# Two tiles for the first K^T V, one undivided last copy, and a different chunk order in one product

## Chip, cores, metric

One core of one Trainium2 chip. The metric is the device time of one execution in microseconds (us). The kernel before took 285.2 us (median of 3 runs, 285.11 to 285.89). Matrix products are in bf16, inputs and outputs in fp32. Medians below are of all runs listed; ratios are the mean time of one kernel's fast runs over the mean of the other's fast runs of the same rounds, so not quite the ratio of the medians that are quoted.

## The reference

Linear attention without softmax, a norm per head, then a two-layer product with ELU between:

```python
kv  = np.einsum('bhsd,bhse->bhde', k, v)          # q, k, v: 8 x 8 x 576 x 64
out = np.einsum('bhsd,bhde->bhse', q, kv)
rms = np.sqrt(np.mean(out * out, axis=-1, keepdims=True) + 1e-06)
x   = (out / rms * g_norm)  # -> transposed to 4608 x 512
h   = x @ w_in                                     # 512 x 2048
g   = np.where(h > 0, h, np.exp(np.minimum(h, 0)) - 1)
return g @ w_out                                   # 2048 x 512
```

## The kernel before

Tokens go in nine groups of 512 (NT = 9, groups 0 to 8). The four chunks of 128 rows that make up a group's x^T are called chunks 0 to 3; each holds two heads. A, V are ACT and DVE. PSUM is handed out by tags: "A" and "B" are one pair of banks each, "m" is a pool of two single banks, "x" another one of two. An allocation from a pool whose buffers are all taken waits for the last reader of the buffer it gets.

The start of batch 0 (cuts marked):

```python
    def chunk_kv(kv_ps, c):
        kv_mm(0, [kv_ps[:, s, :] for s in range(2)], c % 2, (c // 2,))

    def chunk_kv_out(kv_ps, c, eng):
        rows, cols = slice(c // 2 * 64, c // 2 * 64 + 64), slice(c % 2 * 64, c % 2 * 64 + 64)
        copy_on(eng, kv_sb[rows, 0, c % 2], kv_ps[rows, :, cols])
    # ...
    g_ps = pair("A", "g_ps")
    kv_ps = pair("B", "kv_ps")
    # ... first casts; transposed q in a tile of "m"
    mean = pair("A", "mean")[:, 0, :]
    chunk_kv(kv_ps, 0)
    chunk_kv_out(kv_ps, 0, V)
    chunk_kv(kv_ps, 2)
    chunk_kv_out(kv_ps, 2, V)
    chunk_y(0, single("x", "y_ps"))
    chunk_square(0)
    idle(1, mean)                      # filler matmul, keeps the tensor engine busy
    chunk_y(2, single("x", "y_ps"))
    chunk_square(2)
    idle(1, mean)
    mean_mm(sq0[0], mean)
    r = r_tile()
    inv_t(r[:, 0, :], mean)            # Ln, then Exp, on ACT
    ps = turned_q(0, 1, "m")
    q_t_out(0, 1, V, ps, slice(0, 8))
    mean = single("m", "mean")
    mean_mm(sq0[2], mean)
    nc.scalar.activation(r[:, 1, :], mean, AF.Ln, bias=eps_col)
    kv_ps = pair("B", "kv_ps")
    h_ps = [pair("A", "h_ps")]
    chunk_kv(kv_ps, 1)
    # ...
```

Group 1's first products, and the tail. `mm1` runs `mm1_part` over all four chunks for its two tiles, then the ELU; `last_columns` computes the last 128 rows of the output in two halves of 256 columns:

```python
    for i, tag in enumerate("mBAmBAm"):
        if i < 4:
            mm1(1, i, tag)()
    # ...
    def last_columns():
        for n in range(2):
            cols = slice(n * 256, n * 256 + 256)
            ps = single("m", "o_ps")[:, 0:256]
            # ... 16 matmuls into ps
            o = outp.tile([P, 2, DM], FP32, name="o_sb", tag="o")[:, 0, 0:256]
            if n == 0:
                nc.scalar.copy(o, ps)
            else:
                nc.scalar.copy(o[:, 0:128], ps[:, 0:128])
                nc.vector.tensor_copy(out=o[:, 128:256], in_=ps[:, 128:256])
            last_store(J - 1, o, cols)     # one store from ACT's queue, one from SyncE's
```

Of the kernel before, what the change touches and what calls it, by code (L numbers as in the profile page):

```python
# [16 lines left out]
def kernel(  # L17
# [13 lines left out]
    nc = tc.nc  # L31
# [11 lines left out]
    V, A, Q = nc.vector, nc.scalar, nc.gpsimd  # L43
# [64 lines left out]
    def copy_on(eng, out_, in_):  # L108
        if eng is nc.scalar:
            nc.scalar.copy(out_, in_)  # L110
        else:
            eng.tensor_copy(out=out_, in_=in_)  # L112
# [16 lines left out]
    def single(tag, name):  # L129
        pool = ps_x if tag == "x" else ps_m2  # L130
        return pool.tile([P, 512], FP32, name=name, tag=tag)

    def pair(tag, name):
        if tag in ("x", "m", "mx"):
            return [single(t, name) for t in (tag + tag)[:2]]
        return ps_m1.tile([P, 2, 512], FP32, name=name, tag=tag)
# [14 lines left out]
    def kv_mm(b, kv_ps, u, ls=range(2)):  # L151
        for j in range(RK):
            for s in range(2):
                rows = slice(s * 64, s * 64 + 64)
                for l in ls:
                    nc.tensor.matmul(  # L156
                        kv_ps[s][l * 64 : l * 64 + 64, u * 64 : u * 64 + 64],
                        lhsT=bf["k", b][rows, 2 * l + u, j, :],
                        rhs=bf["v", b][rows, 2 * l + u, j, :],
                        start=(j == 0),  # L160
                        stop=(j == RK - 1),
                    )
# [180 lines left out]
    def elu(T, i, ps, relu):  # L343

        parts = [(0, 2, ps)]
        if isinstance(ps, list):
            parts = [(a, a + 1, ps[a].unsqueeze(1)) for a in range(2)]
        e = mlpt.tile([P, 2, G], BF16, name="elu_e", tag="elu_e")
        for lo, hi, h in parts:
            nc.scalar.activation(e[:, lo:hi, :], h, AF.Exp)  # L350

        def freed():
            r = mlpt.tile([P, 2, G], BF16, name="elu_h", tag="elu_h", bufs=2)
            for lo, hi, h in parts:
                nc.scalar.activation(r[:, lo:hi, :], h, AF.Relu)  # L355
            parts[:] = [(0, 2, r)]

        if relu and relu != "later":
            freed()

        def rest():
            nc.vector.tensor_scalar(  # L362
                out=e, in0=e, scalar1=1.0, scalar2=1.0, op0=ALU.min, op1=ALU.subtract
            )
            for lo, hi, h in parts:
                nc.vector.tensor_tensor(  # L366
                    out=gT[T][:, 2 * i + lo : 2 * i + hi, :],
                    in0=e[:, lo:hi, :],
                    in1=h,
                    op=ALU.add if relu else ALU.max,  # L370
                )

        return (freed, rest) if relu == "later" else rest

    def g_tile(T):
        gT[T] = mlpg.tile([P, FC, G], BF16, name="gT", tag="gT")

    def mm1_part(T, i, ps, cs, cols=slice(0, 512), last=True):
        for a in range(2):
            f = 2 * i + a  # L380
            for n, c in enumerate(cs):
                nc.tensor.matmul(  # L382
                    (ps[a] if isinstance(ps, list) else ps[:, a, :])[:, cols],
                    lhsT=w_in_sb[:, c, f * P : f * P + P],
                    rhs=xT[T][:, c, cols],
                    start=(c == 0),
                    stop=(last and n == len(cs) - 1),
                )

    def mm1(T, i, tag, relu=False):  # L390
        if i == 0:
            g_tile(T)
        ps = pair(tag, "h_ps")
        mm1_part(T, i, ps, range(KC))
        return elu(T, i, ps, relu)
# [27 lines left out]
    def last_store(j, o, cols):  # L423
        rows = out_dram.rearrange("(b p j) f -> b p j f", b=B, j=RK)
        for h, eng in enumerate((nc.scalar, nc.sync)):
            b, jj = slot_of(NT - 1, 2 * j + h)
            eng.dma_start(out=rows[b][:, jj, cols], in_=o[h * 64 : h * 64 + 64])
# [5 lines left out]

    def last_columns():

        for n in range(2):
            cols = slice(n * 256, n * 256 + 256)
            ps = single("m", "o_ps")[:, 0:256]
            for f in range(FC):
                nc.tensor.matmul(  # L440
                    ps,
                    lhsT=gT[NT - 1][:, f, (J - 1) * P : J * P],
                    rhs=w_out_sb[:, f, cols],
                    start=(f == 0),
                    stop=(f == FC - 1),
                )
            o = outp.tile([P, 2, DM], FP32, name="o_sb", tag="o")[:, 0, 0:256]
            if n == 0:
                nc.scalar.copy(o, ps)
            else:  # L450
                nc.scalar.copy(o[:, 0:128], ps[:, 0:128])  # L451
                nc.vector.tensor_copy(out=o[:, 128:256], in_=ps[:, 128:256])  # L452
            last_store(J - 1, o, cols)

    def mm2_half(T, i):
# [2 lines left out]
    def store(T, half):  # L458
        rows = out_dram.rearrange("(b p j) f -> b p j f", b=B, j=RK)
        o = o_sb[T, half]  # L460
        for h in range(2):
            hs = slice(h * 64, h * 64 + 64)
            (b0, j0), (b1, j1) = (slot_of(T, 4 * half + 2 * t + h) for t in range(2))
            if b0 == b1:
                nc.sync.dma_start(out=rows[b0][:, j0 : j1 + 1 : 2, :], in_=o[hs])
            else:
                nc.sync.dma_start(out=rows[b0][:, j0, :], in_=o[hs, 0, :])
                nc.sync.dma_start(out=rows[b1][:, j1, :], in_=o[hs, 1, :])
# [62 lines left out]
    def turned_q(b, u, tag):  # L531

        ps = as_bf16(single(tag, "qt_ps"))
        q_t_mm(b, u, range(8), ps)
        return ps

    def first_cast(name, cs, eng, js):
        copy_on(eng, bf[name, 0][:, cs[0] : cs[-1] + 1 : 2, js, :], first[name][:, :, js, :])
# [7 lines that stand above are left out]
# [38 lines left out]
    kv_ps = pair("B", "kv_ps")  # L584
# [5 lines left out]
    ps = turned_q(0, 0, "m")  # L590
# [2 lines left out]
    q_t_out(0, 0, V, ps, slice(0, 8))  # L593
    first_cast("v", (0,), A, high)
    first_cast("v", (0,), V, low)
    mean = pair("A", "mean")[:, 0, :]
    chunk_kv(kv_ps, 0)
    chunk_kv_out(kv_ps, 0, V)
    chunk_kv(kv_ps, 2)
    chunk_kv_out(kv_ps, 2, V)  # L600
    chunk_y(0, single("x", "y_ps"))
# [8 lines left out]
# [7 lines that stand above are left out]
# [14 lines left out]
    mean = single("m", "mean")  # L631
# [34 lines left out]
    for tag, j0 in (("A", 0), ("B", 2)):  # L666
        ps = pair(tag, "o_ps")
# [4 lines left out]
    for u in range(2):  # L672
        n = Turned(1, u)
# [3 lines left out]
        kv_ps = [single("x", "kv_ps") for _ in range(2)]  # L677
# [32 lines left out]
    at = attention(2)  # L710
    freed, rest = {}, {}
    for i, tag in enumerate("mBAmBAm"):
        if i < 4:
            mm1(1, i, tag)()
        else:
            freed[i], rest[i] = mm1(1, i, tag, "later")
        if i == 3:
            at["kv"]()
        if i == 4:
            at["se0"]()  # L720
            freed[4]()
            at["sum0"]()
            at["inv0"]()
        if i == 5:
            at["mul0"]()
            store(0, 0)
            freed[5]()
        if i == 6:
            rest[4]()
            rest[5]()  # L730
    ps = pair("B", "h_ps")
# [13 lines left out]
    ps = pair("A", "o_ps")  # L745
# [61 lines left out]
    for i in (1, 3, 4, 5):  # L807
        mm2_half(NT - 1, i)
    last_columns()


# [28 lines left out]
```

## Time and profile before

| | before |
|---|---|
| time, median of 3 | 285.2 us |
| span of the profiled execution | 283.3 us, granted clock 1.0 |
| tensor engine busy | 97% of the span |
| share of the tensor engine in the chain that ended last | 96% |

The first rows of the profile's page give the busy time of each engine. The chain that ended last is followed back from the end; an engine that is nearly all of the chain can only be helped where it stands still. The lines for this are in the prediction below.

### The profile page before, as it was taken

The page shows a single profiled execution, that of the slowest core. Times are in us where ns is not written, and L with a number is a line of the kernel's source. Part 1 is how long each engine was busy: PE and PEld are TensorE (multiplying, and loading weights), DVE is VectorE, ACT ScalarE, POOL GpSimd, SP SyncE. Part 2 cuts the span into 40 slices and gives each one's busy share as a digit, 9 for nine tenths or more (in the row PEclk, how much of TensorE's full clock was granted, in tenths as well). Part 3 has the DMA queues.
Part 4 walks back from the last instruction along what each step waited for, and adds up shares of the span by engine and source line. Part 5 has one row for each costly group of instructions (what it writes and reads, how often), then busy time and mean ns, then how long its engine had stood idle before and what let it go on. Part 6 is the DMA issues. An engine that isn't in the chain of part 4 may idle for free.

```text
span 283.3 us, 5120 instructions
## 1 busy us (share of the span) xinstructions
PE 274.8 (97%) x2089; PEld 129.5 (46%) x2123; DVE 164.3 (58%) x222; ACT 141.4 (50%) x210; POOL 49.9 (18%) x89
## 2 busy tenths in 40 slices
PE   8899999999999999999999999999999999999994
PEld 3444444444544444444444444444444444444443
DVE  2459532867578647655775478537872787344600
ACT  3688359594667355425542555245533553333321
POOL 7743303332340033033003310000000000000000
PEclk9999999999999999999999999999999999999999
DMA  7999999999995979579627961602150235020222
GB/s 211 193 204 206 207 257 235 211 257 177 206 253 92 155 220 226 65 188 258 155 29 174 266 158 40 166 13 74 39 111 0 74 39 111 0 76 0 74 74 75
DMA packets 50571, 39.46 MB, mean 139 GB/s; under 512 B 30964, under 2 KB 44020, under 8 KB 50548
## 3 DMA queue, kind: packets, MB, share of 16 engines
q0 software_dynamic: 15008, 21.30, 37.4%
q1 hardware_dynamic: 35136, 17.31, 29.1%
q10 hardware_dynamic: 404, 0.53, 0.5%
q8 instruction: 16, 0.26, 0.4%
q14 instruction: 7, 0.06, 0.1%
HBM read 36.70 MB, written 9.44 MB: 163 GB/s over the span
## 4 chain that ended last, share of the span: by engine, by line
PE 96%; DVE 1%; issue 1%; ACT 1%
PE o_ps L403 43%; PE h_ps L382 42%; PE at L250 2%; PE kv_ps L529 2%; PE at L156 2%; PE o_ps L440 1%; PE h_ps L573 1%; PE qt_ps L174 1%; PE kv_ps L156 1%; PE mean L199 1%; PE y_ps L189 1%; DVE kv_sb L112 0%; DVE xT L212 0%; DVE qT L112 0%; ACT rT L634 0%
## 5 line engine op out<-in xcount | busy, mean ns | idle before, releaser
L403 PE MATMUL o_ps<-w_out_sb,gT 128*128 128x512 bf16 x548 | 128.8, 379 | 0.7 <-issue 0.2
L382 PE MATMUL h_ps<-xT,w_in_sb 128*128 128x512 bf16 (+1 forms) x540 | 126.6, 376 | 1.0
L350 ACT ACTIVATE elu_e<-h_ps 128x1024 bf16<-128x1024 f32 (+1 forms) x79 | 74.0, 952 | 89.4 <-PE h_ps L382 78.6
L403 PEld LDWEIGHTS <-gT 128*128 128x128 bf16 x560 | 54.4, 98 | 65.5 <-issue 0.4
L382 PEld LDWEIGHTS <-w_in_sb 128*128 128x128 bf16 x560 | 53.2, 98 | 61.3 <-issue 0.4
L366 DVE TENSOR_TENSOR gT<-elu_e,h_ps 128x1024 bf16<-128x1024 bf16 (+1 forms) x67 | 77.2, 1157 | 6.6
L362 DVE TENSOR_SCALAR elu_e<-elu_e 128x1024 bf16<-128x1024 bf16 x72 | 30.9, 430 | 65.0 <-ACT elu_e L350 64.8
L419 ACT COPY o_sb<-o_ps 128x512 f32<-128x512 f32 x32 | 18.3, 586 | 20.9 <-PE o_ps L403 20.2
L103 POOL CAST q_bf<-st_q 128x384 bf16<-128x384 f32 x36 | 18.5, 558 | 39.0 <-DMA st_q<-in_q_dram 33.6
L283 DVE TENSOR_REDUCE ss<-sq 128x16 f32<-128x1024 bf16 x14 | 17.1, 1219 | 6.8 <-ACT sq L277 6.8
L299 DVE TENSOR_TENSOR xs<-at,ss 128x1024 bf16<-128x1024 f32 x14 | 17.1, 1220 | 1.9 <-ACT ss L292 1.9
L277 ACT ACTIVATE sq<-at 128x1024 bf16<-128x1024 f32 x14 | 14.4, 1029 | 0.0
L212 DVE SCALAR_TENSOR_TENSOR xT<-y_ps,g_col,rT 128x512 bf16<-128x512 f32 (+1 forms) x10 | 6.2, 640 | 10.0 <-ACT rT L209 7.9
L339 POOL COPY gate<-qT 1x16 bf16<-1x16 bf16 x5 | 1.1, 218 | 57.7 <-DMA qT<-q_bf 57.7
L355 ACT ACTIVATE elu_h<-h_ps 128x1024 bf16<-128x1024 f32 (+1 forms) x12 | 9.3, 817 | 0.0
L90 POOL DMA_DIRECT2D v_bf<-in_v_dram x11 | 7.8, 713 | 4.2 <-DMA w_in_sb<-in_moe_w_in_dram 2.1
L156 PEld LDWEIGHTS <-k_bf 64*64 64x64 bf16 x576 | 6.4, 107 | 4.6 <-issue 4.1
L90 POOL DMA_DIRECT2D k_bf<-in_k_dram x11 | 7.7, 703 | 3.0 <-DMA w_in_sb<-in_moe_w_in_dram 2.3
L312 DVE TENSOR_SCALAR xT<-xT,g_col 128x1024 bf16<-128x1024 bf16 x14 | 6.7, 481 | 2.2 <-DMA xT<-xs 2.2
L250 PEld LDWEIGHTS <-qT 64*128 64x128 bf16 (+1 forms) x248 | 4.3, 97 | 6.1 <-issue 5.9
L366 DVE TENSOR_TENSOR gT<-elu_e,elu_h 128x1024 bf16<-128x1024 bf16 x9 | 6.6, 736 | 0.8
L452 DVE COPY o_sb<-o_ps 128x128 f32<-128x128 f32 x1 | 0.3, 292 | 11.3 <-ACT o_sb L451 11.3
(60 smaller groups left out, 102.4 us busy)
## 6 DMA issues: line engine op xcount, KB each, us to landing
st_q<-in_q_dram POOLq DMA_DIRECT2D x6, 1152.0 KB, 8.3
out_dram<-o_sb SPq DMA_DIRECT2D x24, 256.0 KB, 3.4
k_bf<-in_k_dram POOLq DMA_DIRECT2D x6, 576.0 KB, 10.3
v_bf<-in_v_dram POOLq DMA_DIRECT2D x6, 576.0 KB, 12.9
out_dram<-o_sb SPq DMA_DIRECT2D x19, 128.0 KB, 2.4
w_out_sb<-in_moe_w_out_dram POOLq DMA_DIRECT2D x4, 512.0 KB, 15.0
w_in_sb<-in_moe_w_in_dram POOLq DMA_DIRECT2D x2, 512.0 KB, 11.0
q_bf<-in_q_dram POOLq DMA_DIRECT2D x3, 288.0 KB, 13.4
```

Of the source, the lines that this page charges most:

```text
L90: eng.dma_start(out=dst.rearrange("p m j d -> p m (j d)"), in_=in_[:, ms, :])
L103: nc.gpsimd.tensor_copy(out=bf["q", b][:, u, js], in_=raw[b][:, u::2, js, :].rearrange("p l j d -> p j l d"),)
L156: nc.tensor.matmul(kv_ps[s][l * 64 : l * 64 + 64, u * 64 : u * 64 + 64], lhsT=bf["k", b][rows, 2 * l + u, j, :], rhs=bf["v", b][rows, 2 * ...
L277: nc.scalar.activation(sq, st["se", h], AF.Square)
L283: nc.vector.reduce_sum(out=ss, in_=st.pop(("sq", h)).rearrange("p l (m e) -> p (l m) e", e=D), axis=AX.X,)
L299: nc.vector.tensor_tensor(out=st["xs"][:, 2 * h : 2 * h + 2, :].rearrange("p i (l m e) -> p l i m e", l=2, e=D), in0=se_ps.rearrange("p l ...
L350: nc.scalar.activation(e[:, lo:hi, :], h, AF.Exp)
L362: nc.vector.tensor_scalar(out=e, in0=e, scalar1=1.0, scalar2=1.0, op0=ALU.min, op1=ALU.subtract)
L366: nc.vector.tensor_tensor(out=gT[T][:, 2 * i + lo : 2 * i + hi, :], in0=e[:, lo:hi, :], in1=h, op=ALU.add if relu else ALU.max,)
L382: nc.tensor.matmul((ps[a] if isinstance(ps, list) else ps[:, a, :])[:, cols], lhsT=w_in_sb[:, c, f * P : f * P + P], rhs=xT[T][:, c, cols] ...
L403: nc.tensor.matmul(o_ps[T, j], lhsT=gT[T][:, f, j * P : j * P + P], rhs=w_out_sb[:, f, :], start=(f == 0), stop=(f == FC - 1),)
L419: nc.scalar.copy(o_sb[T, half][:, j % 2, :], o_ps[T, j])
```

## The change

Its intent: (1) chunks 0 and 2 of K^T V get a tile each, so that chunk 2 need not wait for chunk 0's copy; the mean moves to pool "m" to make room. (2) Group 1's first product takes chunk 3, which is ready last, last for both of its tiles. (3) The last copy is one DVE copy of 256 columns, instead of 128 on ACT and 128 on DVE, which ran one after the other.

```diff
-        for n in range(2):
+        for n, eng in enumerate((A, V)):
 ...
-            if n == 0:
-                nc.scalar.copy(o, ps)
-            else:
-                nc.scalar.copy(o[:, 0:128], ps[:, 0:128])
-                nc.vector.tensor_copy(out=o[:, 128:256], in_=ps[:, 128:256])
+            copy_on(eng, o, ps)
 ...
-    mean = pair("A", "mean")[:, 0, :]
+    mean = single("m", "mean")
     chunk_kv(kv_ps, 0)
     chunk_kv_out(kv_ps, 0, V)
+    kv_ps = pair("A", "kv_ps")
     chunk_kv(kv_ps, 2)
 ...
-        if i < 4:
+        if i == 0:
+            g_tile(1)
+            ps = pair(tag, "h_ps")
+            mm1_part(1, 0, ps, (0, 2, 1), last=False)
+            mm1_part(1, 0, ps, (3,))
+            elu(1, 0, ps, False)()
+        elif i < 4:
             mm1(1, i, tag)()
```

## The prediction

> **What bounds the kernel now.** I read the page's busy shares first, then the chain that ended last, then that chain piece by piece in time at the three places the change touches: the start (7.8 to 20 us), the hand-over to group 1 (46 us) and the tail (after 279 us).
>
> ```profile
> PE 274.8 (97%) x2089; PEld 129.5 (46%) x2123; DVE 164.3 (58%) x222; ACT 141.4 (50%) x210; POOL 49.9 (18%) x89
> ...
> PE 96%; DVE 1%; issue 1%; ACT 1%
> ```
>
> The tensor engine is the chain for 96% of the span, at a granted clock of 9 tenths or more in every slice. No matmul of the real products is removed, and the instruction order on it is the same in both kernels apart from one block of eight matmuls. So only places where it stands still on the chain, and the tail after it, can give time. The chain by time names them; columns are start, duration and what:
>
> ```profile
> 7.85 0.48 PE kv_ps L156 x18
> 8.33 0.02 issue
> 8.36 0.29 DVE kv_sb L112
> 8.65 0.04 issue
> 8.69 0.38 PE kv_ps L156 x13
> ...
> 9.20 0.30 DVE kv_sb L112
> 9.51 0.10 issue
> 9.60 0.40 PE y_ps L189 x2
> 10.01 0.32 PE mean L529
> 10.33 0.21 PE mean L199
> 10.54 0.57 PE qt_ps L174 x16
> 11.11 0.32 PE mean L199
> 11.44 0.40 PE kv_ps L156 x18
> ...
> 46.49 0.65 PE h_ps L382 x3
> 47.14 0.01 issue
> 47.15 3.83 PE h_ps L382 x17
> ...
> 279.35 0.27 ACT o_sb L451
> 279.62 0.02 issue
> 279.64 0.29 DVE o_sb L452
> ```
>
> At 8.33 chunk 2's K^T V waits until chunk 0's result has been copied out of the same tile, 8.69 - 8.33 = 0.36 us. At 46.49, three matmuls of group 1's first product run and the fourth comes only at 47.15. The three start 216 ns apart (46.33, 46.54, 46.76 in the timeline), so the fourth was due at 46.98: 0.17 us lost to the last chunk of xT, whose scaling on DVE runs 46.34 + 0.75 = 47.09. After the last matmul, the two halves of the last copy run one after the other, not side by side: ACT 279.35 to 279.62, then DVE 279.64 to 279.94. The line of the DVE half says so:
>
> ```profile
> L452 DVE COPY o_sb<-o_ps 128x128 f32<-128x128 f32 x1 | 0.3, 292 | 11.3 <-ACT o_sb L451 11.3
> ```
>
> [...] between a full-array matmul at 11.04 and the 64x64 ones at 11.36 lie 0.32 us where 0.216 would do. This matters below. [...]
>
> **Part 1, different tiles at the start.** Removed: the wait of 0.36 us. Chunk 2's products can follow chunk 0's at about 8.16 (they issue 16 ns apart, the last of chunk 0 at 8.12) and end at 8.63 instead of 9.16; their inputs are there, as the queue's waits show the last of these two loads landed before 7.88. But not all of the 0.53 reaches the next steps:
> - y of chunk 0 now waits itself for the copy ending at 8.64, so starts at 8.69 instead of 8.88 and 8.97 for its two halves; it ends at 9.09 instead of 9.35, gain about 0.27. ACT's first square starts at 9.13 instead of 9.39.
> - The filler matmul behind it, and the change of tiling mode after that, hold y of chunk 2: start to start the old distances are 0.31 (8.97 to the filler's weights at 9.28) and about 0.32 (filler to 9.60), so y of chunk 2 comes at about 9.33 instead of 9.60, although its operand is ready at about 9.0.
> - The second filler and the first mean keep their distance: the mean at 9.90 instead of 10.165. Its Ln on ACT starts at 10.32 instead of 10.58 and ends, after 0.69, at 11.00 to 11.01 instead of 11.27.
>
> Now the new wait. The mean used to live in the pair A; A now holds chunk 2's product, so the mean takes a slot of the two-buffer pool "m". In order of allocation that pool gets: transposed q, mean 0, transposed q, mean of chunk 2. With two slots the fourth takes mean 0's slot and must wait until its Ln has read it. Released at about 11.00, plus about 0.04 to reach the tensor engine (the hop from DVE at 8.65 shows 0.04), it starts at 11.04. Before, the same matmul started at 11.04, in its place in the order. The transposes in front of it come 0.27 us early and then the tensor engine stands still for about that long. From there the next K^T V (11.36), its copy (11.88), y of chunk 1 (12.30) and the rest up to the first product at 19.86 are as before. So I put Part 1 at 0.00 us, with -0.05 to +0.12 as what the small hops leave open.
>
> **Part 2, the last chunk last.** Six matmuls without chunk 3, instead of three, run ahead: 46.33 + 6 x 0.216 = 47.63 is when the chunk is first needed, and it is ready at 47.14. The stall of 0.17 us goes. ACT's first exponential is at 48.11 before because ACT is copying o_ps until then (four copies from 46.21, 2.03 us); the first tile is done at about 47.63 + 0.38 = 48.01, so ACT loses nothing. The following products have slots free: pair B is copied out by 47.2 and A by 48.25, needed at about 48.06 and 49.8. From 47.15 on the chain is tensor-engine work with only 0.05 us pieces of issue, so the gain should reach the end: 0.17 us.
>
> **Part 3, the undivided copy.** Before: 279.35 to 279.94 = 0.59 us for two copies in series. After: one DVE copy of 128x256. [...] The hop from the tensor engine to DVE is 0.03 (8.33 to 8.36), the same as to ACT (279.32 to 279.35). Gain 0.59 - 0.425 = 0.16 us. The stores follow the copy in both kernels: issue at 279.97, landing and closing to 283.3, a fixed 3.3 us which shifts as a whole. The output slot's earlier stores had been waited for by 275.8, well ahead.
>
> **Sum.** 0.00 + 0.17 + 0.16 = 0.33 us off 285.2: 284.87, rounded to 284.9.
>
> **Rivals.** (a) The start pays in full: if mean 2 did not wait for the Ln, the 0.27 us that the mean gains would go through, or 0.36, the whole removed wait; then 284.5 to 284.6. For it: the wait is on the chain. Against: the slot order above, and Ln's own 0.69 us behind the first mean. (b) The start gets worse: the new wait releases later than I think, or the following K^T V waits twice, and mean 2 comes at 11.1 or 11.2: 285.0. For it: ACT's three instructions before that point follow each other almost without gaps. Against: y of chunk 0 is early by a wait that I read from the trace. (c) The gain at 47 us is given back: ACT's exponential of the first tile comes later, the m slots come free later, and a later product in m waits. Those two slots are read by DVE until 51.08, the next user comes at about 51.7, so 0.6 us is spare; if it still happened, 285.05. (d) DMA arrivals fix the start: chunk 3's v has landed by 12.55 at the latest and the first w_in pieces are used at about 13.9; they could swallow an earlier start but not cause a loss. It would make (a) smaller only.
>
> **Range and chances.** The three runs before spread from 285.11 to 285.89, more than the whole gain, so the median itself carries some 0.2 us. With the parts' spread (start -0.05 to +0.27, hand-over 0 to 0.2, tail 0.1 to 0.2) I take 284.5 to 285.3. Two per cent is 5.7 us; all the standing still at the three places adds up to 0.36 + 0.17 + 0.59 = 1.1 us, so neither a gain nor a loss of 2% is in reach: 0.01 and 0.01.
>
> **What would show it.** In the changed profile: chunk 2's K^T V at about 8.16 with no wait for DVE; y of chunk 0 at 8.69 and of chunk 2 at about 9.33; the second mean's matmul at about 11.04 with the tensor engine waiting for ACT's Ln in front of it, and the next K^T V at about 11.36 as before; eight matmuls 216 ns apart from about 46.33 with no wait for xT; one DVE copy of about 0.43 us at the end, and from its end to the span's end what it was before (283.3 - 279.94 = 3.36 us). I am wrong on Part 1 if the second mean starts before 10.95 or after 11.1, on Part 2 if the product after the block is not 0.17 earlier relative to its start, on Part 3 if the copy takes under 0.35 or over 0.5 us. A span of 282.95 or so (283.3 less 0.33) is the whole in one number.

The sum came to 0.00 + 0.17 + 0.16 = 0.33 us off 285.2, that is 284.9. Its 0.16 is 0.59 - 0.425, and 0.425 stands as the estimate, which no run had shown; the copy then took 425 ns in the changed kernel. The change of tiling mode stands with what the trace before shows: 0.32 us from the start of a 128x128 matmul to that of a 64x64 one (11.04 to 11.36), against 0.216 between the 128x128 ones at 46.33, 46.54 and 46.76.

## The result, and the profile after

The changed kernel took **285.42 us** (median of 6 runs, 284.91 to 286.71). In the same rounds the kernel before took 285.4 us (6 runs, 285.11 to 286.11). The ratio is 1.0004, 95% interval 0.9979 to 1.0028: the same. The predicted 284.9 us was missed, and the median lies outside the range of 284.5 to 285.3.

The profiled execution of the changed kernel happened to be its longest, 286.71 us with a span of 284.9, at a granted clock of 0.998; so the two profiles differ by 1.67 us while the medians do not. The first two lines of the page's parts on busy time and on the chain:

```profile
PE 276.2 (97%) x2123; PEld 128.9 (45%) x2123; DVE 164.9 (58%) x222; ACT 141.2 (50%) x209; POOL 49.2 (17%) x89
...
PE 88%; DMA 4%; ACT 3%; DVE 3%; issue 0%; SPq 0%; DVEq 0%
```

One ACT instruction is gone (210 to 209): the halved copy. The tensor engine's share of the chain fell from 96 to 88%; DMA, ACT and DVE took 10% between them. Following both traces side by side at the same instructions gives the account of the 1.67 us:

| place | after minus before |
|---|---|
| arrival of the first loads | +0.02 us |
| start, up to the first product (Part 1) | +0.01 |
| hand-over to group 1, 46 us (Part 2) | -0.17 |
| wait for x^T of group 2, 70 to 73 us | +1.57 |
| tail, from the last matmul to the end of the copy (Part 3) | +0.24 |

**Start.** The chain of the changed kernel from 7.8 us; columns are start, duration, what:

```profile
7.87 0.48 PE kv_ps L156 x24
8.35 0.02 issue
8.38 0.29 DVE kv_sb L112
8.67 0.04 issue
8.71 0.40 PE y_ps L189 x2
9.12 0.32 PE mean L525
...
10.35 0.70 ACT rT L208
11.04 0.04 issue
11.09 0.38 PE mean L199
11.46 0.40 PE kv_ps L156 x18
...
16.61 3.27 PE h_ps L569 x14
19.88 2.20 PE h_ps L382 x10
```

The wait between the two K^T V is gone, and y of chunk 0 starts at 8.71. But ahead of the second mean, at 11.09, the chain now goes through ACT's Ln, and from there everything is where it was.

**Hand-over.** The chain of the changed kernel at 46 us:

```profile
44.79 1.73 PE o_ps L403 x8
46.52 6.91 PE h_ps L382 x32
```

Where the chain before was broken after three matmuls, one piece of 32 follows.

**The wait at 70 us.** What the engines wait for between 60 and 74 us; columns are engine, written tile, line, releaser, then us in total, times, longest. Only the lines that concern xT are shown, first of the kernel before, then of the changed one:

```profile
DVE xT L312 <- DMA xT<-xs: 1.4, 1, 1.4
```

```profile
DVE xT L312 <- DMA xT<-xs: 3.1, 2, 1.8
PE h_ps L382 <- DVE xT L312: 1.2, 1, 1.2
PEld L382 <- DMA xT<-xs: 1.0, 1, 1.0
```

In the second, the transposed x of group 2 lands late, and the tensor engine waits for it, once through DVE and once directly. This is the largest difference of the two profiles, and no part of the change touches that place. Is it the change's doing?

**Tail.** The chain of the changed kernel at its end:

```profile
277.24 1.76 PE o_ps L440 x16
279.00 0.02 issue
279.02 0.38 ACT o_sb L110
279.41 0.02 issue
279.42 1.77 DMA out_dram<-o_sb
281.19 0.42 DVE o_sb L112
```

The undivided copy takes 0.42 us as predicted, but the last matmul (not in this chain) ended at 280.74, and the copy starts only at 281.18. The profile says that it waited for a store. That cannot be right: the first half's two stores land at 281.35 and 281.63, after the copy has started. Before, last matmul to end of copies was 0.63 us; now it is 0.87.

### The profile page after: what moved, and what is told of

Its sections match the earlier page's. It is cut to its first block, busy times and chain, and to the rows that moved or that the text cites. A ratio compares the mean times of both kernels' runs of the same rounds, so it can differ in the third digit from the quotient of the medians.

```text
span 284.9 us, 5151 instructions
## 1 busy us (share of the span) xinstructions
PE 276.2 (97%) x2123; PEld 128.9 (45%) x2123; DVE 164.9 (58%) x222; ACT 141.2 (50%) x209; POOL 49.2 (17%) x89
## 4 chain that ended last, share of the span: by engine, by line
PE 88%; DMA 4%; ACT 3%; DVE 3%; issue 0%; SPq 0%; DVEq 0%
PE h_ps L382 40%; PE o_ps L403 40%; DMA first_v<-in_v_dram 2%; DMA xT<-xs 2%; PE at L250 2%; PE at L156 1%; PE h_ps L569 1%; ACT elu_e L350 1%; DVE ss L283 1%; PE kv_ps L156 1%; PE y_ps L189 1%; ACT sq L277 1%; PE mean L199 1%; DMA out_dram<-o_sb 1%; PE o_ps L440 1%; PE qt_ps L174 0%
## 5 line engine op out<-in xcount | busy, mean ns | idle before, releaser
L382 PE MATMUL h_ps<-xT,w_in_sb 128*128 128x512 bf16 (+1 forms) x560 | 128.0, 376 | 1.3 <-DVE xT L312 1.2
L362 DVE TENSOR_SCALAR elu_e<-elu_e 128x1024 bf16<-128x1024 bf16 x72 | 31.7, 440 | 64.4 <-ACT elu_e L350 64.4
## 6 DMA issues: line engine op xcount, KB each, us to landing
k_bf<-in_k_dram POOLq DMA_DIRECT2D x6, 576.0 KB, 10.8
```

Of the source, the lines that this page charges most:

```text
L362: nc.vector.tensor_scalar(out=e, in0=e, scalar1=1.0, scalar2=1.0, op0=ALU.min, op1=ALU.subtract)
L382: nc.tensor.matmul((ps[a] if isinstance(ps, list) else ps[:, a, :])[:, cols], lhsT=w_in_sb[:, c, f * P : f * P + P], rhs=xT[T][:, c, cols] ...
```

## The experiments

Because the 70 us wait moves whole-kernel times by up to 2.7 us from run to run, segments of the traces decide, and the times are given for completeness. "Tail" is the end of the last matmul to the end of the last copy.

### Undoing one part each

Four kernels, each the changed kernel with one edit, in 5 rounds (the kernel before there: median 286.41 us, 284.97 to 287.44).

`e1_old_tail` puts the old divided copy back:

```diff
-            copy_on(eng, o, ps)
+            if n == 0: nc.scalar.copy(o, ps)
+            else: ...128 columns on ACT, then 128 on DVE, as before
```

> Changed kernel with the old divided last copy (parts 1 and 2 only). My theory: the tail of the changed kernel costs 0.24 us more than before, because the wait for the tensor engine stands in a separate wait instruction ahead of the DVE copy and the copy starts 0.44 us after the last matmul's end instead of 0.04. Then here, from the last matmul's end to the last copy's end 0.63 us as in the kernel before (0.87 in the changed one), and the time about 0.17 us below the kernel before (285.0 to 285.3 if that is at 285.3). Rival (the tail is innocent and the part 2 gain does not last): the tail again 0.8 us or more, or the same time as the changed kernel. Either way, how long the tensor engine waits at about 71 us for the transposed xT (0 before, 1.4 us in the changed kernel's profile) is a sample of whether this varies from run to run.

Measured: 285.29 us, ratio 0.9973 (0.9944 to 1.0003). Tail 0.627 us, as in the kernel before (0.626).

`e2_last_act` gives the undivided copy to ACT:

```diff
-        for n, eng in enumerate((A, V)):
+        for n, eng in enumerate((A, A)):
```

> Changed kernel with the undivided last copy on ACT instead of DVE. My theory (the wait's place, not the undividing, costs): ACT has the tensor engine's wait in the copy itself, so it starts 0.04 us after the last matmul's end and takes 0.37 us: 0.41 us from the last matmul's end to the copy's end, against 0.87 in the changed kernel and 0.63 before; time 0.46 us below the changed kernel. Rival 1 (the copy waits for the store of the first half, as the profile's release says): the copy would start 1.7 to 1.8 us after the first half's stores are issued, so again some 0.4 us after the last matmul. Rival 2 (a DVE start after 11 us of standing still is slow): also 0.41 us here.

Measured: 285.64 us, ratio 0.9979 (0.995 to 1.0007). Tail 0.408 us, the figure that the theory and both rivals gave, so this run does not tell them apart. The line of its last copy in the timeline (start, duration, engine, line, operation, idle before and releaser):

```profile
281.85 0.37 ACT L110 COPY o_sb<-o_ps 128x256 f32<-128x256 f32 x1 [1.38 <-PE o_ps L440]
```

It starts 0.04 us after the last matmul's end. Undividing the copy is therefore worth 0.22 us of the tail, where the copying engine (here ACT) starts at once. With DVE it is the late start that loses it.

`e3_own_tile` gives the second half a buffer of its own, so that no earlier store has to be waited for:

```diff
+    o_last = const.tile([P, 256], FP32, name="o_last")
 ...
-            o = outp.tile(...)[:, 0, 0:256]
+            o = outp.tile(...)[:, 0, 0:256] if n == 0 else o_last
```

> Changed kernel, the last copy undivided on DVE but into a tile of its own, so that its only wait is for the tensor engine and sits in the copy itself. My theory: it starts 0.04 us after the last matmul's end and takes 0.425 us: 0.46 us against 0.87 in the changed kernel, the 0.16 us gain that I predicted. Rival 2 (DVE is slow to start after standing still for 11 us, whatever it waits for): 0.8 to 0.9 us as in the changed kernel.

Measured: 285.37 us, ratio 0.9975 (0.9948 to 1.0002). Tail 0.461 us, the predicted one, although DVE had stood idle for 11.04 us: a slow start after idling (rival 2) is ruled out. The chain's releaser is now the tensor engine:

```profile
279.60 0.42 DVE L113 COPY o_last<-o_ps 128x256 f32<-128x256 f32 x1 [11.04 <-PE o_ps L441]
```

From the copy's end to the end of the span it took 3.53 us, though, against 3.33 in the changed kernel: 0.20 was given back behind the copy, so that nothing was won against the kernel before (0.461 + 3.53 = 3.99 us from the last matmul's end to the end of the span, before 0.626 + 3.33 = 3.96).

`e4_mean_in_A` takes the new slot wait away: the mean goes back into A, which is free once chunk 2's result has been copied out:

```diff
     chunk_kv_out(kv_ps, 2, V)
+    mean = pair("A", "mean")[:, 0, :]      # and no longer single("m", "mean")
```

> Changed kernel with the first mean back in the pair A, allocated after chunk 2's copy has left it, so that the second mean takes a free slot of m. My theory of part 1 (the slot wait ate the whole 0.27 us): the second mean's matmul starts at about 10.8 us instead of 11.09, with no wait for the Ln, and everything up to the hand-over at 46 us comes 0.25 to 0.3 us earlier than in the changed kernel. Rival (something else at the start, the arrival of chunk 3's v or of w_in, sets the later times): the second mean earlier, but y of chunk 1 or of chunk 3 and the first product no earlier than in the changed kernel.

Measured: 285.56 us, ratio 0.9982 (0.9955 to 1.001). The timeline of the tensor engine around the second mean, with start and duration first:

```profile
10.57 0.39 PE L199 MATMUL mean<-sq,ones 128*128 128x512 bf16 x1
10.89 0.47 PE L156 MATMUL kv_ps<-v_bf,k_bf 64*64 64x64 bf16 x18
11.83 0.40 PE L189 MATMUL y_ps<-qT,kv_sb 64*64 64x512 bf16 x2
```

The second mean stands at 10.57 (10.8 was expected) instead of 11.09, and no wait is noted for it. At the 100th weight load, counted from the first product's, the trace is 0.26 us ahead of the kernel before; the changed kernel is 0.01 behind. So the slot wait of the prediction was real and ate the whole gain of Part 1. But between the start and 46 us the 0.26 went again, against the expectation: about 0.10 of it by 16.3 us, where the products of L569 start when w_in has landed (a weight load waits 0.7 us for it), and 0.20 at 32.84 us. The chain of this kernel there:

```profile
17.28 15.52 DMA w_out_sb<-in_moe_w_out_dram
32.80 0.04 issue
32.84 0.38 PE o_ps L403
```

The first products with w_out run from 28.0 us; the one at 32.84 is the first that needs the second of w_out's four loads (issued at 17.28), and it starts when that load has landed, at 32.80. In the first profiles of the kernel before and of the changed kernel the same product starts at 33.00 and 33.02, and the load had landed at 32.80 and 32.82. At most 0.2 us can be won there, whatever the start gains: what rival (d) of the prediction said of arrivals, though for a load that it did not name.

### Repeats, the tail alone, and a best version

5 rounds, the kernel before again (285.61 us, 284.85 to 286.34). `rep_before` and `rep_after` are unchanged copies of the two kernels; `best_act` is `e4_mean_in_A` with ACT's undivided copy; `e5_tail_alone` is the kernel before with only Part 3 (a single look).

> The kernel before, unchanged, once more, for a second profile of it. So far the wait of the tensor engine for xT of group 2 at 70 to 73 us was, against the kernel before's first profile: 1.57 us in the changed kernel, 0.07 less than nothing with the old tail, 2.7, none and 0.7 in the other three, although all of these have the same instructions up to there but for the start. Theory: this wait varies from execution to execution with the transfers and belongs to the kernel before as well; then this profile can show anything from 0 to 2.7 us there and the times spread over 2 us again. Rival (the change brings the wait about): 0.2 us or less here.

> The changed kernel, unchanged, once more. Tail theory: again about 0.87 us from the last matmul's end to the copy's end, the copy starting 0.4 us or more after the wait instruction has ended. Time against the kernel before: by the parts 0.00 - 0.17 + 0.24 = 0.07 us more, not to be seen in times that spread over 2 us. The wait at 70 to 73 us anything from 0 to 2.7 us if it varies by itself.

> The mean back in the pair A after chunk 2's copy, the hand-over as changed, and the last copy undivided on ACT. From the earlier runs: start 0.25 us earlier of which the arrival of w_out at about 32.8 us leaves up to 0.17 to 0.2, hand-over 0.17, tail 0.63 - 0.41 = 0.22: together 0.55 to 0.6 us below the kernel before in the segments that do not depend on the transfers, and about as much in the lowest of its times. Rival (the start gain is all taken by arrivals): 0.4 us.

> The kernel before with the undivided last copy on DVE and nothing else. Tail theory: from the last matmul's end to the copy's end 0.87 us (0.63 before), so this part alone costs 0.24 us. My prediction had been 0.46. Rival (the tail is long only together with the other two parts): 0.46. At the start and the hand-over it should stand as the kernel before: second mean at 11.04 to 11.06, the stall of 0.17 us in front of the last chunk.

Measured: `rep_before` 285.05 us (ratio 0.999, 0.9963 to 1.0017), `rep_after` 285.5 (1.0005, 0.9979 to 1.003), `best_act` 285.24 (0.9993, 0.9965 to 1.0021), `e5_tail_alone` 286.52. Even the kernel before against itself came out at 285.05 and 285.61, so times this close tell nothing.

The waits of `rep_before` between 60 and 74 us, again those for xT alone:

```profile
DVE xT L312 <- DMA xT<-xs: 2.9, 2, 1.8
PE h_ps L382 <- DVE xT L312: 1.2, 1, 1.2
PEld L382 <- DMA xT<-xs: 1.0, 1, 1.0
```

They are those of the changed kernel's first profile, in the unchanged kernel. The length of this stretch, against the first profile of the kernel before, was +1.33 us in `rep_before`, +1.38 in `e5_tail_alone`, +1.57 and +0.19 in two profiles of the changed kernel, and between -0.07 and +2.66 in the other variants. It varies by execution in both kernels, so it does not need the change; whether the change makes it likelier, two profiles of each cannot tell. What makes the transposes land late in some executions stays open.

`e5_tail_alone` has a tail of 0.870 us, `rep_after` too: the loss belongs to Part 3 alone, and the three traces agree to 0.001 us. `best_act` has a tail of 0.410, the hand-over 0.17 us shorter, and a start 0.26 us ahead, all of which was gone by 46 us (0.28 us lost). Hand-over and tail together are about 0.4 us, the rival's figure; the expected 0.55 to 0.6 was missed. Its lowest run, 284.48 us, is the lowest of all, but its ratio does not tell it from the kernel before.

### Why does DVE start late?

In the changed kernel, the condition that the last matmul has ended is not in the copy but in a separate wait instruction ahead of it, together with that of an earlier store, because the output buffer is reused. The trace has three such wait instructions ahead of this copy, which begin at 268.55, 277.11 and 277.20 us. The last one ends at 280.78, 0.05 us after the last matmul, and the copy starts 0.40 us after that. My first theory was that a separate wait instruction costs DVE these 0.40 us. The rival was that DVE, idle for 11 us, wakes slowly, which `e3_own_tile` speaks against already.

`e7_two_waits` is `e3_own_tile` with a small ACT write into the same buffer, which gives the copy two engines to wait for; `e8_two_waits_awake` keeps DVE busy with four small copies as well:

```diff
+            if n == 0:
+                for t in range(4):      # e8 only
+                    nc.vector.tensor_copy(out=awake[:, t, :], in_=o[:, 0:128])
+                nc.scalar.copy(o_last[:, 0:1], eps_col)
```

> The own-tile version of the last DVE copy with one wait added: ACT writes one column of that tile earlier, so the copy waits for the tensor engine and for ACT (the latter long fulfilled), with no wait for a store, and the list of waits puts the tensor engine's in a separate instruction again. Theory (the separate wait costs on DVE): 0.85 to 0.9 us from the last matmul's end to the copy's end. Rival (the waits for the stores, or the reused slot, cost): 0.46 us as with the own tile alone.

> As the run before, and DVE has four small copies from the first half to do until about a microsecond before the end, so it has not stood still for 11 us when the wait comes. Theory (the separate wait by itself costs about 0.4 us on DVE): again 0.85 to 0.9 us. Rival (it is DVE's long standing still that makes the start after a separate wait slow): about 0.5 us.

Measured (the kernel before 286.36): 286.82 and 285.99 us. Tails 0.531 and 0.532; the copy starts 0.04 us after the separate wait. Both theories fall: a separate wait costs 0.07 us against the copy that waits itself (0.461), and being awake changes nothing.

Next theory: a wait instruction that holds two conditions. `e9_three_waits` adds a small load into the buffer, `e10_dma_and_pe` has the load without ACT's write, and `e11_early_load` has both long before the end:

```diff
+    nc.sync.dma_start(out=o_last[0:1, 64:128], in_=...g_norm)   # e11: ahead of the last group's second products
+    nc.scalar.copy(o_last[:, 0:1], eps_col)                     # not in e10
```

> My theory that any separate wait costs 0.4 us on DVE fell: with one wait moved out, the copy ended 0.53 us after the last matmul's end, against 0.46 with none and 0.87 in the changed kernel. New theory: the 0.4 us come when the wait instruction ahead holds two semaphores, a store's or load's and the tensor engine's, as in the changed kernel. Here the own-tile copy gets a third wait, for a small load into the same tile early on, so that one wait instruction with two semaphores (the load's and the tensor engine's) stands ahead and the ACT one stays in the copy: 0.85 to 0.9 us if the pairing costs. Rival A (three wait instructions in a row cost): 0.53 us, as there is only one here. Rival B (the reused slot, that is the stores of an earlier tile or the profile's release by a store): 0.53 us.

> As the run before without ACT's write, so the copy waits for the small load (in a separate wait instruction, long fulfilled) and for the tensor engine (in the copy itself). Both theories: 0.46 us from the last matmul's end to the copy's end; 0.5 or more would mean that any wait instruction ahead of the copy costs, even one fulfilled long before.

> The run e9 with the small load and ACT's write moved ahead of the last 80 or so products, so that the load has landed many microseconds before and the paired wait (load and tensor engine) lasts for microseconds on its second half, as in the changed kernel (3.58 us there, only 0.20 in e9). If the long paired wait is what makes DVE slow to go on: 0.85 to 0.9 us from the last matmul's end to the copy's end. If it is the reused slot with its five waits for stores: 0.52 us again.

Measured: 286.79 and 286.09 us (the kernel before 287.45), and 287.2. Tails 0.518, 0.464 and 0.518. In `e9_three_waits` and `e11_early_load` a wait instruction holds two conditions, and in the latter it stands for 12.2 us; the copy still starts 0.04 us after it. This theory falls too.

`e13_absorb` puts a tiny DVE write into the same reused buffer just ahead of the copy; `e6_dve_awake` puts four small copies into another buffer there:

```diff
+            if n == 1:
+                nc.vector.memset(o[:, 0:1], 0.0)                                    # e13
+                for t in range(4):                                                  # e6
+                    nc.vector.tensor_copy(out=awake[:, t, :], in_=first[:, 0:128])
```

> The changed kernel, with one tiny write by DVE into the last copy's slot ahead of it, which takes over the five waits for stores and the one for ACT; the copy is left with the tensor engine's wait and one for DVE's own write. If the wait list of the copy is the cause: 0.46 to 0.53 us from the last matmul's end to the copy's end, in the same reused slot. If the slot itself is: 0.85 to 0.9.

> The changed kernel with four small DVE copies from the first half ahead of the last copy. They take over ACT's wait, so the list keeps the five waits for stores in separate instructions and leaves the tensor engine's in the copy itself. If where the tensor engine's wait stands decides: 0.46 us. If the stores' waits or the reused slot decide: 0.85 to 0.9 us.

Measured: 286.43 and 286.46 us. Tails 0.461 and 0.464, with the reused buffer. In `e13_absorb` the tiny write now starts 0.43 us after the wait ahead of it, at 277.75 instead of 277.32, where it harms nothing. So the reuse of the buffer is not the cause; the delay stays near the same place of DVE's program, whatever instruction stands there.

Two last kernels separate kind from place. `e14_five_loads` has its own buffer, but five loads into it that give three wait instructions of the same kinds, so that the copy stands at the same place. `e15_shifted` is the changed kernel, with its waits and its buffer, and five tiny DVE writes some 11 us earlier, so that the copy stands five places further on:

```diff
+    for t in range(5):                                                                  # e14, on e3
+        nc.sync.dma_start(out=o_last[t : t + 1, 64:128], in_=...g_norm)
+    nc.scalar.copy(o_last[:, 0:1], eps_col)

+    for t in range(5):                                                                  # e15, on the changed kernel
+        nc.vector.memset(shift[:, t : t + 1], 0.0)
```

> The last copy in its own tile, with five small early loads and an early ACT write into that tile, so that its list is of the same kind as in the changed kernel: five transfers, the tensor engine, ACT, that is three wait instructions in a row ahead of it, but no reused slot and no stores. If three wait instructions in a row make DVE slow: 0.85 to 0.9 us from the last matmul's end to the copy's end. If the reused slot does: 0.52 us.

> The changed kernel with five tiny DVE writes to an unused tile earlier, which need nothing and only move the last copy five places down DVE's program; waits and slot as in the changed kernel. If the list of waits decides: 0.87 us again. If the copy's place in the program [...] decides: 0.5 us or so, the gap of 0.4 us behind the last wait instruction gone or behind another instruction.

Measured: 287.66 and 286.33 us (the kernel before 285.62). Tails **0.870** and **0.516**. The timeline's lines of the copy in the changed kernel, in `e14_five_loads` and in `e15_shifted`:

```profile
281.18 0.42 DVE L112 COPY o_sb<-o_ps 128x256 f32<-128x256 f32 x1 [11.45 <-DMA out_dram<-o_sb]
```

```profile
281.94 0.42 DVE L113 COPY o_last<-o_ps 128x256 f32<-128x256 f32 x1 [11.45 <-DMA out_dram<-o_sb]
```

```profile
280.79 0.42 DVE L113 COPY o_sb<-o_ps 128x256 f32<-128x256 f32 x1 [11.06 <-PE o_ps L441]
```

The second reads as if a store released a copy into a buffer that no store has used. The stores in question landed at 282.12 and 282.40 us, after the copy had started at 281.94; the releaser is an inference of the profile, and a wrong one there.

The trace's records of DVE, numbered in order of time with waits included (read from the packed trace; the views shown here leave the waits out), show what the slow cases share:

| kernel | record number of the copy | separate wait to copy | tail | copy end to span end |
|---|---|---|---|---|
| after, `rep_after`, `e5_tail_alone` | 320 | 0.40 | 0.870 | 3.33 (after) |
| `e4_mean_in_A` | 320 | 0.41 | 0.886 | 3.32 |
| `e14_five_loads` | 320 | 0.40 | 0.870 | 3.52 |
| `e7_two_waits` | 318 | 0.04 | 0.531 | 4.02 |
| `e9_three_waits`, `e11_early_load` | 318 | 0.04 | 0.518 | 3.74 |
| `e10_dma_and_pe` | 318 | (in the copy) | 0.464 | 3.78 |
| `e3_own_tile` | 317 | (in the copy) | 0.461 | 3.53 |
| `e8_two_waits_awake` | 322 | 0.04 | 0.532 | 3.34 |
| `e13_absorb` | 322 | (in the copy) | 0.461 | 3.34 |
| `e6_dve_awake` | 324 | (in the copy) | 0.464 | 3.33 |
| `e15_shifted` | 325 | 0.04 | 0.516 | 3.34 |

Where record 320 comes right behind a separate wait, it starts 0.40 to 0.43 us after it, be it the copy or the tiny write of `e13_absorb`; copies at 318, 322 and 325 start after 0.04. In `e3_own_tile`, where the copy is record 317, record 320 falls into the closing sequence, and the cost turns up there: it begins 0.45 us after the one before it, against 0.09 for the same pair in `e13_absorb`. And in the kernel before, DVE's half copy was record 320 as well, but it waited for ACT's half at that time, so nothing showed. The order of time is not quite that of the program: waits and instructions overlap, and in `e6_dve_awake` and `e8_two_waits_awake`, where record 320 is one of the small copies, no late start is seen.

What is at that place? The DMA view, by queue (packets, MB, share of the engines' time), has a packet of the queue that it calls "instruction" near it; such a packet is called a fetch here. The changed kernel between 281.4 and 283 us, then `e15_shifted` between 269 and 270.5 us:

```profile
q14 instruction: 1, 0.01, 1.5%
```

```profile
q14 instruction: 1, 0.01, 2.3%
```

In the kernels whose record 320 is the late copy, the fetch starts 0.64 to 0.69 us after it (281.87 in the changed kernel), and in `e13_absorb` 0.63 us after the tiny write. So what is late cannot have waited for this very fetch; the two come one after the other. `e15_shifted` has none between 281.3 and 283: the fetch moved with the record, to 269.63, where record 320 is one of the tiny writes. The delay moved too: the wait instruction behind these writes begins 0.54 us after record 316 there (269.02 and 268.47), 0.04 in the changed kernel. (How much of it is the issue of five writes, no run separates.)

Where nothing shows as late, the fetch comes while DVE waits anyway: in the kernel before at 276.88, 1.07 us after the last separate wait, while the half copy waits until 279.64; in the two kernels with small copies at 269.83 (`e6_dve_awake`) and 269.28 (`e8_two_waits_awake`), while DVE waits for ACT until 279 us.

In the changed kernel three of the 8,192-byte fetches of this queue come at 46.35, 153.66 and 281.87 us, near DVE's records 65, 193 and 320: about 128 records apart. The queue has four more of that size in the execution (49.16, 86.09, 170.09 and 173.02 us), which this count does not place; the trace does not say for which engine a fetch is. That the fetch and the delay go together, and move together, is shown: with the copy at record 320 the copy starts 0.40 us after the wait, with five writes ahead of it 0.04, and the fetch comes at 269.63 instead of 281.87. What makes DVE late at that place is not shown.

The last column of the table has a second cost, which goes together with the fetch as well. In the four kernels with the copy at 318 it takes 3.74 to 4.02 us from the copy's end to the end of the span, against 3.33. Their fetch falls among the packets of the last two stores (in `e7_two_waits` from 282.18 to 282.86, the first of these packets at 282.18), and one of the 16 pieces of each store lands 0.45 to 0.74 us after the other fifteen; in all other kernels the last piece is at most 0.05 us behind, and the fetch falls elsewhere. What holds this piece up, the trace does not show. (The 3.52 of `e14_five_loads` has another reason: behind the last landing SyncE goes through seven waits there instead of four, 0.06 us each.)

## Why the prediction was wrong

**Part 1, right: 0.00 predicted, +0.01 found.** The new wait came where the slot order said it would: second mean at 11.09 (predicted 11.04), next K^T V at 11.39 (11.36), first product at 19.88 (19.86). (What happens when two engines use one bank at once was not put to the test: the two chunks were in different banks, or waited.) `e4_mean_in_A` shows that the slot was the reason: without it the start is 0.26 us ahead, the 0.27 of rival (a). Rival (a) would still not have held for the time, since the arrivals of w_in and w_out took it back.

**Part 2, right: -0.17 predicted, -0.17 found.** It is -0.17 in all kernels with that block of eight matmuls, 0.00 in those without.

**Part 3, wrong: -0.16 predicted, +0.24 found.** The copy was sized rightly (0.425). The step that failed is "The hop from the tensor engine to DVE is 0.03 (8.33 to 8.36), the same as to ACT (279.32 to 279.35)." That hop was read from a copy which carried its own wait. The last copy's wait was moved into a separate instruction (some 0.05 us) and the copy stood at the place in DVE's program where 0.40 us go by. Together 0.445 us instead of 0.03. The tail would have been as predicted in `e3_own_tile`, `e6_dve_awake` and `e13_absorb` (0.461 to 0.464), though the first gives 0.20 us back behind the copy, where the prediction had "a fixed 3.3 us which shifts as a whole". What the divided copy had hidden, the undivided one laid bare.

**The sum.** With +0.24 in place of -0.16, the sum is 0.00 - 0.17 + 0.24 = +0.07 us instead of -0.33; the medians of the same rounds differ by 0.02, and the ratio of 1.0004 is 0.1 us. Of the 0.52 us by which 284.9 was missed, this step is 0.40; the base is another 0.2 (285.2 was a median of three runs, 285.4 of six), and the rest, some 0.1 the other way, is within the scatter.

**The range** was too narrow. It counted on 0.2 us for the median; one stall at 70 us alone varies by up to 2.7 us between executions, in both kernels, and the single profile read before, with 1.4 us of DVE's waiting there, could not show that.

## What to carry to other kernels

Before an undivided instruction replaces two in series at the end of a program, ask where its wait stands: in the instruction, or in separate ones ahead of it (here 0.05 to 0.07 us more: tails of 0.516 to 0.532 against 0.461 to 0.464). Ask also at which place of the engine's program it stands, and try it a few places further on: here 0.40 us went by ahead of the copy at DVE's record 320, and 0.04 at 325. Waiting for another engine may have been hiding that: in the kernel before, the half copy was record 320 too, but waited for ACT's half until 279.64, and nothing showed. A wait that is removed by a new buffer is worth only as much as the next wait leaves: here first a pool's slot, then a load. And where parts are worth 0.2 us in a kernel that scatters by 2, compare segments of traces, not times, and take a releaser named by the profile for a guess until its own time fits.
